# Attention with mixture-of-experts routing: reciprocals brought across partitions by a product, q scaled while it is split, loads, stores and scatters at other places of a pair, last routing in other banks

## The chip, the cores and the metric

One core of a Trainium2 chip runs the whole program. The metric is the device time of one execution, in microseconds (us); the time of a kernel is the median of its runs. Five engines work beside each other: PE (TensorE), DVE (VectorE), ACT (ScalarE), POOL (GpSimd) and SP (SyncE), which here only issues DMAs. Each engine takes its instructions strictly in the order of its own list.

## The reference

```
scores = scale * q @ k.T + bias(|i - j|, i)      # 8 batches x 8 heads, 576 x 576, head size 64
attn   = exp(scores - max) / (sum + 1e-9)
x      = (attn @ v), as 4608 tokens x 512        # token = (batch, position), heads side by side
logits = x @ w_gate + modality_bias[modality]    # 8 experts
e      = argmax(logits); g = softmax(logits)[e]
out    = g * (relu(x @ w1[e]) @ w2[e])           # 512 -> 1024 -> 512, the token's own expert
```

All is float32. The kernel splits operands into a high part (fp32r) and the rest, and adds three products.

## The kernel before, in words

**Stages.** A first stage of about 78 us builds the bias table. Then `attention` goes over 32 pairs of heads (four pairs make a batch), up to about 625 us. Then `moe_first` and `moe_rest` multiply tiles of 256 tokens by their expert's weights, in a phase of products with w1 and one with w2.

**A pair.** `ORDER` is a table of five strings, the stages 0 to 4 of a pair's turn n; `attention` carries the words out in that order, and this order in the program is the order on each engine. A `+` means pair n+1, `++` pair n+2, a `-` pair n-1. `S` issues score products of 128 queries (`scores`), `E` the exponentials on ACT, `T` transposes, `A` products with v, `R` and `N` the remaining 64 positions, `C` a copy on POOL that keeps them (L458). A capital starts a step on PE and the small letter copies its banks out. `L` issues the q and k loads on SP (L359, L363), `Q` is `scale_q`, which multiplies q by -1/8 in place on POOL (L386), `V` loads v (L372, L378). `P` transposes q and k on PE into the banks `x`, `H` writes the high part on ACT (`high`), `G` the rest on DVE (`low`). The remaining 64 rows of q, in `QD`, already take the factor -1/8 in `high` and `low` (L336, L343), while the other rows are copied with factor 1 (L334, L341).

**Routing beside attention.** From stage 2 of every fourth turn (n = 5, 9, 13, ...) the words `Y`, `X` and `O` carry out a batch's steps of `route_steps`, one batch behind. `s_recip` takes reciprocals of the softmax sums (`rs`, DVE) and spreads them over `rec` by POOL copies (L771, L776). The sums of the last 64 positions lie for one head of a pair in partitions 64 to 127 and are wanted in 0 to 63: POOL copies them to `mv` (L778), SP issues a DMA from `mv` to `mv2` (L780), and POOL copies `mv2` into `rec` (L798). `s_logits` multiplies by the gate's weights (L790, into `eps`, copied out at L327 and L329), `s_logits_t` transposes the result into the banks `x`, and DVE multiplies it by `rec` (L814, `lw`). `s_rows` transposes x rows into the banks `x`; ACT and DVE copy them to one of two row buffers `xrb`, POOL multiplies by `rec` (L905), and `D` (`route_store`) has SP store them to `xg` in DRAM (L946). `s_scatter`, by the word `Z`, is an indirect DMA from POOL that writes token numbers to `tab` (L922), five for each batch. A scatter waits until the one before has landed.

**Routing beside experts.** The last batch's routing runs in `moe_first`, between products. Its banks `x` are `xps`, which are also two of the three banks `p2` that the second phase of a tile (L1283) and the transposes of the next tile's rows (`xprep`, L1247) take in turn. Two other banks, `pq`, are used by `tiny` in `moe_rest` alone.

Of the kernel before, what the change touches and what calls it, by code (L numbers as in the profile page):

```python
# [11 lines left out]
F32 = mybir.dt.float32  # L12
# [4 lines left out]
ALU = mybir.AluOpType  # L17
# [4 lines left out]
P = 128  # L22
S = 576
D = 64
H = 8
NP = H // 2
HID = 32
S4 = S // 4
HS = S // 2
E = 8  # L30
DM = H * D
# [78 lines left out]
class Attn:  # L110
# [269 lines left out]

    SC = float(-1.0 / np.sqrt(np.float32(D)))

    def scale_q(self, n):

        x = self.qraw[n].rearrange("p c h d -> p (c h d)")
        self.nc.gpsimd.tensor_scalar(x, x, self.SC, None, op0=ALU.mult)  # L386

    def prep(self, n, part, u="x"):

        QK, QD, bk = self.QK[n % 2], self.QD[n % 2], self.banks[u]  # L390
        if part < 2:
            x = (self.qraw, self.kraw)[part].pop(n)
            for j in range(4):
                self.turn(bk, 64 * j, x[:, j, :, :].rearrange("p h d -> p (h d)"))
            hi, lo = (QK[:, part, a, 0:512].rearrange("p (j r w) -> p j r w", j=4, r=2) for a in range(2))
            return [
                (bk[r][:, 0:256].rearrange("p (j w) -> p j w", j=4), hi[:, :, r], lo[:, :, r], 1.0) for r in range(2)
            ]
        x = self.qkrem[n % 2]
        self.turn(bk, 256, x[:, 0, :])  # L400
        self.nc.tensor.transpose(bk[0][:, 320:384], x[0:64, 1, :], self.idf[0:64, 0:64])
        out = [(bk[r][:, 256:320], QD[:, 0, 64 * r : 64 * r + 64], QD[:, 1, 64 * r : 64 * r + 64], self.SC) for r in range(2)]
        return out + [(bk[0][:, 320:384], QK[:, 1, 0, 512:S], QK[:, 1, 1, 512:S], 1.0)]
# [138 lines left out]
    def first_steps(self, route):  # L542


        out = {}

        def add(blk, f):
            out.setdefault(blk, []).append(f)

        def pe(k):  # L550
            evac[k] = self.prep(0, k)

        def split(parts):
            for x in parts:
                self.high(*x)
                self.low(*x)

        evac = {}
        add(0, lambda: self.load_qk(0))
        add(self.V0, lambda: self.load_v(0))  # L560
        add(self.TG1[0], lambda: self.nc.sync.dma_start(self.tg1, self.io["c_tg1"]))
        add(self.TG1[1], lambda: self.nc.scalar.activation(self.tg1, self.tg1, AF.Copy, scale=self.w1c[:, 0:1]))
        add(self.PREP0[0] - 2, lambda: self.scale_q(0))
        for blk, k in zip(self.PREP0, (0, 1, 2)):
            add(blk, lambda k=k: pe(k))
            add(blk + 1, lambda k=k: split(evac.pop(k)))
        if self.n_pair > 1:
            loads = self.qk_loads(1)
            for blk in self.QK1:
                add(blk, lambda: next(loads, None))  # L570
        for blk in self.ROUTE:
            add(blk, lambda: next(route, None))
        return out
# [4 lines left out]


    ORDER = (  # L580
# [5 lines left out]
    )  # L586

    def attention(self):
        n_pair = self.n_pair
        tail = self.first_tiles() if self.K else {}  # L590
        for at in self.ROUTE_LATE:
            tail.setdefault(at, []).append(lambda: next(self.route, None))
        for u, k in self.LATE:
            tail.setdefault((0, u), []).append(lambda k=k: next(self.late[k], None))
        self.bg = None
        scored, evac = {}, {}
        half = lambda k: lambda u: [(u, b, k) for b in range(2)]
        bank = lambda k: lambda u: [(u[0], int(u[1]), k)]
        high = lambda u: half(1)(u) + half(2)(u)
        both = self.both = lambda u: half(0)(u) + high(u)  # L600
        steps = {
            "T": (self.etrans, lambda u, c: half(0)(u) if c == 4 else both(u)),
            "R": (self.rtrans, high),
            "N": (self.rtrans4, bank(2)),
            "A": (self.av, lambda u, k: bank(0)(u)),
            "P": (self.prep, lambda u, k: (high if k == 2 else half(0))(u)),
        }

        def start(k, n, *a):
            f, parts = steps[k]  # L610
            self.hold((k, n, *a[:-1]), parts(a[-1], *a[:-1]))
            evac[(k, n, *a[:-1])] = f(n, *a)

        def end(k, n, *a):
            a, by = (a[:-1], ["av".index(a[-1])]) if a and isinstance(a[-1], str) else (a, [])
            evac.pop((k, n, *a))(*by)
            del self.held[k, n, *a]

        def low(n, k):
            for x in evac.pop(("P", n, k)):  # L620
                self.low(*x)
            del self.held["P", n, k]

        pair = {
            "S": lambda n, c: scored.update({(n, c): self.scores(n, c)}),
            "E": lambda n, c: self.exps(*scored[n, c].pop(0)),
            "C": self.compact,
            "H": lambda n, k: [self.high(*x) for x in evac["P", n, k]],
            "G": low,
            "Q": self.scale_q,  # L630
            "V": lambda n: n in self.vmain or self.load_v(n),
            "L": self.load_qk,
        }
        for k in steps:
            pair[k] = lambda *a, k=k: start(k, *a)
            pair[k.lower()] = lambda *a, k=k: end(k, *a)
        for n in range(n_pair + 2):
            for u in range(5):
                for f in tail.get((n, u), ()):
                    f()  # L640
                if u == 2 and n > 1 and n % NP == 1:
                    assert self.route_done()
                    self.bg = self.route_steps(n // NP - 1)
                for op in self.ORDER[u].split():
                    op, _, to = op.partition(":")
                    m = n + op.count("+") - op.count("-")
                    if op == "D":
                        self.route_store()
                    elif op == "Z":
                        self.route_scatter()  # L650
                    elif op in ("X", "Y", "O"):
                        self.route_next(op, to)
                    elif op in ("x", "y"):
                        self.route_evac(op.upper())
                    elif 0 <= m < n_pair and not (n > n_pair and op[0] in "CV"):
                        pair[op[0]](m, *(int(x) for x in op[1:].strip("+-")), *([to] if to else []))
        while self.scatters:
            self.route_scatter()
# [96 lines left out]
    def route_steps(self, b):  # L755
        nc, rt = self.nc, self.rt
        xT = [self.xT[NP * b + p] for p in range(NP)]
        sums = [self.sums.pop(NP * b + p) for p in range(NP)]
        rec, oh = self.rec, self.oh
        C5 = [P, 5, E]  # L760
        st = {}
# [4 lines left out]
        def s_recip():  # L766
            rs = rt.tile([P, NP, 9], F32, tag="rs", name=f"rs{b}")
            for p in range(NP):
                nc.vector.tensor_scalar(rs[:, p, :], sums[p], 1e-9, None, op0=ALU.add)
            nc.vector.reciprocal(rs, rs)  # L770
            nc.gpsimd.tensor_copy(  # L771
                rec[:, 0:4, :].rearrange("p c (n h) -> p c n h", h=2),
                rs[:, :, 0:8].rearrange("p n (c h) -> p c n h", h=2),
            )
            r4 = rec[:, 4, :].rearrange("p (n h) -> p h n", h=2)
            nc.gpsimd.tensor_copy(r4[0:64, 0, :], rs[0:64, :, 8])  # L776
            mv = rt.tile([P, NP], F32, tag="mv", name=f"mv{b}")
            nc.gpsimd.tensor_copy(mv, rs[:, :, 8])  # L778
            mv2 = rt.tile([64, NP], F32, tag="mv2", name=f"mv2{b}")
            nc.sync.dma_start(mv2, mv[64:P, :])  # L780
            st["mv2"] = mv2

        def s_logits(u):
            st["lt"] = self.lt if b == self.B - 1 else next(self.xr_next)
# [3 lines left out]
            for cols, ps, _ in parts:  # L788
                for p in range(NP):
# [5 lines left out]
                        stop=True,  # L795
                        tile_position=(0, 32 * p),
                    )
            nc.gpsimd.tensor_copy(rec[0:64, 4, :].rearrange("p (n h) -> p h n", h=2)[:, 1, :], st["mv2"])  # L798

            def out():  # L800
                for k, (_, ps, dst) in enumerate(parts):
                    self.copy(k, dst, ps)

            return out

# [221 lines left out]
    def moe_tiles(self, st):  # L1027
# [6 lines left out]
        self.mo = [mp.tile([P, DM], F32, name=f"mo{k}") for k in range(2)]  # L1034
        pp = st.enter_context(tc.tile_pool(name="mps", bufs=1, space=PSUM))
        self.p1 = [pp.tile([P, 2, TS], F32, name=f"p1{k}") for k in range(3)]
        self.pq = [pp.tile([P, DM], F32, name=f"pq{k}") for k in range(2)]
        self.p2 = [pp.tile([P, DM], F32, name="p2")] + self.xps
        self.at = {"p2": -1}

# [609 lines left out]
```

## Time and profile before

| | |
|---|---|
| median of 3 runs | 1106.6 us (1103.4 to 1108.98) |
| the profiled execution, its own time | 1111.95 us |
| its span, first to last instruction | 1110.2 us, granted PE clock 0.970 |
| PE busy | 1018.1 us (92%) |
| DVE, ACT, POOL busy | 748.0 (67%), 683.5 (62%), 266.3 us (24%) |

A PE that is busy 92% of the span leaves some 90 us in which it waited. The profile lists instructions by their line in the program, what an engine waited for before an instruction ("idle before, releaser"), and the clock that PE was granted, where 1.00 is 2.4 GHz and 0.50 is 1.2 GHz.

### The profile page before, as it was taken

Reading aid. Unit: us, or ns where it says so; the run is one execution under the profiler, and the core shown is the slowest. Engines: PE = TensorE matmul, PEld = TensorE weight load, DVE = VectorE, ACT = ScalarE, POOL = GpSimd, SP = SyncE. Lnnn points to the kernel's source line nnn. Section 1 sums busy time; section 2 is a strip of 40 time slices with the busy share of each in tenths; the row PEclk is TensorE's granted clock in tenths of the full one; section 3 lists DMA queues with packets and bytes.
Section 4 is the critical chain, followed back from the end, with each engine's and each line's share of the span. In section 5 each row is a group of like instructions: output and inputs, shape, how many; then the busy total and the mean of one; then the engine's idle time right before and its main releaser. Section 6 shows DMA issues by size and latency. Waiting matters only on the chain. (4 is left out here: it accounts for less than half of the span.)

```text
span 1110.2 us, 30041 instructions
## 1 busy us (share of the span) xinstructions
PE 1018.1 (92%) x11590; PEld 853.6 (77%) x11590; DVE 748.0 (67%) x1777; ACT 683.5 (62%) x1576; POOL 266.3 (24%) x419
## 2 busy tenths in 40 slices
PE   6989999979799798998998888899999999999996
PEld 3447878868688687786876776788978789988995
DVE  7977778858678586886887455777445445565554
ACT  6768778858678576776876544444544445555443
POOL 1012223323233233232323321331302022111120
PEclk9999999989999899898998998999999999999999
DMA  6953222433322332223327101121545712111111
GB/s 173 212 129 75 63 48 75 65 59 105 60 64 61 63 94 49 75 68 66 94 40 221 46 20 39 39 64 48 175 157 190 251 46 63 53 39 48 39 54 36
DMA packets 125677, 93.52 MB, mean 84 GB/s; under 512 B 94737, under 2 KB 103313, under 8 KB 125524
## 3 DMA queue, kind: packets, MB, share of 16 engines
q1 hardware_dynamic: 117908, 71.20, 24.8%
q0 software_dynamic: 7520, 20.30, 6.0%
q8 instruction: 94, 1.54, 0.8%
q14 instruction: 59, 0.48, 0.2%
q10 hardware_dynamic: 96, 0.00, 0.0%
HBM read 141.40 MB, written 19.38 MB: 145 GB/s over the span
## 5 line engine op out<-in xcount | busy, mean ns | idle before, releaser
L453 ACT ACTIVATE Eb<-Eb,mn 128x576 f32<-128x576 f32 x288 | 224.6, 787 | 46.0 <-DVE mn L439 45.8
L439 DVE CUSTOM_DVE_ANT_0 Eb<-sps,NBm 128x576 f32<-128x576 f32 x256 | 183.5, 754 | 21.0 <-PE sps L416 15.3
L416 PE MATMUL sps<-QK 64*128 64x288 f32 x1536 | 153.9, 319 | 11.7 <-ACT QK L334 6.0
L528 PE MATMUL eps<-eT,vraw 128*64 128x144 f32 (+2 forms) x2048 | 158.3, 298 | 6.6 <-ACT eT L327 5.7
L1266 PE MATMUL p<-QK,w1hi 128*128 128x256 f32 x1152 | 162.8, 284 | 1.2 <-ACT w1hi L1239 1.2
L1266 PEld LDWEIGHTS p<-QK,w1hi 128*128 128x128 f32 x1152 | 149.1, 192 | 7.8 <-issue 5.0
L528 PEld LDWEIGHTS eps<-eT,vraw 128*64 128x64 f32 x2048 | 123.3, 140 | 31.9 <-ACT eT L327 16.6
L416 PEld LDWEIGHTS sps<-QK 64*128 64x128 f32 x1536 | 118.2, 193 | 24.7 <-DVE QK L341 10.0
L1269 DVE SCALAR_TENSOR_TENSOR hl<-p,hh 128x512 fp32r<-128x512 f32 x72 | 49.7, 690 | 127.9 <-ACT hh L1268 127.9
L329 DVE COPY eT<-eps 128x512 f32<-128x512 f32 x128 | 87.8, 686 | 49.5 <-PE eps L322 45.7
L1268 ACT ACTIVATE hh<-p 128x512 fp32r<-128x512 f32 x72 | 43.0, 597 | 124.9 <-PE p L1266 112.9
L1292 POOL DMA_INDIRECT out<-mo,idt x36 | 36.5, 1014 | 297.0 <-ACT mo L1291 283.3
L1233 DVE TENSOR_TENSOR w2lo<-NBm,w2hi 128x1024 fp32r<-128x1024 f32 x72 | 89.3, 1240 | 16.2 <-ACT w2hi L1232 16.1
L322 PE MATMUL eps<-idf,Eb 64*128 64x64 f32 x2048 | 94.8, 230 | 4.8 <-ACT xTb L327 1.8
L458 POOL COPY rem<-Eb 128x128 f32<-128x128 f32 x128 | 37.2, 291 | 255.7 <-ACT Eb L453 226.8
L1283 PE MATMUL xps<-w2hi,hh 128*128 128x512 f32 x208 | 86.6, 416 | 7.3 <-DVE NBm L329 3.7
L1266 PE MATMUL p<-QK,w1lo 128*128 128x256 f32 x576 | 92.7, 283 | 0.2 <-DVE w1lo L1240 0.2
L322 PEld LDWEIGHTS eps<-idf,Eb 64*128 64x128 f32 x2048 | 81.8, 143 | 9.8 <-ACT xTb L327 4.3
L1233 DVE TENSOR_TENSOR w1lo<-NBm,w1hi 128x1024 fp32r<-128x1024 f32 x72 | 84.9, 1220 | 3.3 <-ACT w1hi L1232 1.1
L1283 PE MATMUL xps<-w2hi,hl 128*128 128x512 f32 x208 | 84.3, 405 | 0.0
L327 ACT COPY eT<-eps 128x512 f32<-128x512 f32 x128 | 77.4, 605 | 4.6 <-PE eps L322 2.1
L1266 PEld LDWEIGHTS p<-QK,w1lo 128*128 128x128 f32 x576 | 79.4, 192 | 0.6 <-DVE w1lo L1240 0.6
(244 smaller groups left out, 1810.8 us busy)
## 6 DMA issues: line engine op xcount, KB each, us to landing
NBm<-moe_w SPq DMA_DIRECT2D x20, 2048.0 KB
NBm<-moe_w SPq DMA_DIRECT2D x40, 1024.0 KB
NBm<-moe_w SPq DMA_DIRECT2D x32, 512.0 KB
NBm<-xTb SPq DMA_DIRECT2D x32, 288.0 KB
qraw<-q SPq DMA_DIRECT2D x64, 128.0 KB
kraw<-k SPq DMA_DIRECT2D x64, 128.0 KB
vraw<-v SPq DMA_DIRECT2D x32, 256.0 KB
xg<-xrb SPq DMA_DIRECT2D x28, 258.0 KB
```

The costliest lines, as they stand in the source:

```text
L322: self.nc.tensor.transpose(ps[r][0:n, col : col + 64], x[o, :], self.idf[o, o])
L327: self.nc.scalar.copy(out, ps)
L329: self.nc.vector.tensor_copy(out, ps)
L416: nc.tensor.matmul(self.sps[h or 0][:, half, 0:HS], QD[:, a, :] if h is None else QK[o, 0, a, P * c : P * c + P], QK[o, 1, b, ks], start=i ...
L439: nc.vector.tensor_tensor_reduce(out=e.rearrange("p (t w) -> p t w", t=2), in0=ps, in1=nb.rearrange("p (t w) -> p t w", t=2), scale=1.0, s ...
L453: self.nc.scalar.activation(e, e, AF.Exp, bias=mn, scale=-1.0, accum_out=sm)
L528: nc.tensor.matmul(ps[o, :], v[:, h, k, :] if k < 4 else self.vrem[n % 2][:, o], eT[:, h, k, sl] if k < 4 else rT[:, sl], start=k == 0, st ...
L1233: self.nc.vector.tensor_tensor(l, w, h.bitcast(F32), op=ALU.subtract)
L1266: nc.tensor.matmul(ps[:, a, :], w[:, c, fs], x[:, c, :], start=i == 0, stop=i == len(ops) - 1)
L1268: nc.scalar.activation(hh[:, sl, :], ps, AF.Relu)
L1269: nc.vector.scalar_tensor_tensor(hl[:, sl, :], ps, 0.0, hh[:, sl, :].bitcast(F32), op0=ALU.max, op1=ALU.subtract)
L1283: nc.tensor.matmul(ps, h[:, f, sl], m[:, f, :], start=i == 0, stop=i == len(ops) - 1)
```

## The change

`scale_q` is gone; `prep` hands the factor -1/8 for q to `high` and `low`. The word `Q+` in stage 0 is replaced by `L++`, which stood at the head of stage 4. The two `D` of stages 1 and 3 become one at the end of stage 4. `Z` in stage 4 scatters only if all five scatters of a batch are waiting, or in the last turns. `mv`, `mv2` and their copies and DMA are replaced by a product in `s_logits`: columns 64 to 127 of the identity as weights, the four columns of `rs` as the other operand, which puts partitions 64 to 127 into rows 0 to 63 of a bank; DVE copies that into `rec`. In `moe_first` the banks `x` are the two `pq`.

```diff
-    def scale_q(self, n):
-        x = self.qraw[n].rearrange("p c h d -> p (c h d)")
-        self.nc.gpsimd.tensor_scalar(x, x, self.SC, None, op0=ALU.mult)
...
-                (bk[r][:, 0:256].rearrange("p (j w) -> p j w", j=4), hi[:, :, r], lo[:, :, r], 1.0) for r in range(2)
+                (bk[r][:, 0:256].rearrange("p (j w) -> p j w", j=4), hi[:, :, r], lo[:, :, r], (self.SC, 1.0)[part]) for r in range(2)
...
-        add(self.PREP0[0] - 2, lambda: self.scale_q(0))
...
-        "T2-:e t2- S0 Q+ A2--:e0 a2--:a Y:e1 y X:x E0 T3-:e",
-        "x t3- S1 A3--:e0 N-:e1 E0 E1 n- D E1 a3--:v T4-:x R-:x T0:e C0 C1 Z r-:a O",
+        "T2-:e t2- L++ S0 A2--:e0 a2--:a Y:e1 y X:x E0 T3-:e",
+        "x t3- S1 A3--:e0 N-:e1 E0 E1 n- E1 a3--:v T4-:x R-:x T0:e C0 C1 Z r-:a O",
         "t4-:a t0 S2 O A0-:e1 a0-:a E2 P2+:x E2 P0+:x",
-        "H2+ T1:e H0+ V t1 S3 E3 D C2 G0+ A1-:e1",
-        "L++ a1-:v E3 S4 P1+:x H1+ G1+ G2+ O Z C3 O E4",
+        "H2+ T1:e H0+ V t1 S3 E3 C2 G0+ A1-:e1",
+        "a1-:v E3 S4 P1+:x H1+ G1+ G2+ O Z C3 O E4 D",
...
                     elif op == "Z":
-                        self.route_scatter()
+                        if u < 4 or n > n_pair - 3 or len(self.scatters) == 5:
+                            self.route_scatter()
...
-            mv = rt.tile([P, NP], F32, tag="mv", name=f"mv{b}")
-            nc.gpsimd.tensor_copy(mv, rs[:, :, 8])
-            mv2 = rt.tile([64, NP], F32, tag="mv2", name=f"mv2{b}")
-            nc.sync.dma_start(mv2, mv[64:P, :])
-            st["mv2"] = mv2
+            st["rs"] = rs
...
-            nc.gpsimd.tensor_copy(rec[0:64, 4, :].rearrange("p (n h) -> p h n", h=2)[:, 1, :], st["mv2"])
+            odd = self.banks[u[0]][1 - k][0:64, 384 : 384 + NP]
+            nc.tensor.matmul(odd, self.idf[:, 64:P], st["rs"][:, :, 8], start=True, stop=True, tile_position=(0, 0))
+            dst4 = rec[0:64, 4, :].rearrange("p (n h) -> p h n", h=2)[:, 1, :]
...
                     self.copy(k, dst, ps)
+                self.copy(1, dst4, odd)
...
-        self.pq = [pp.tile([P, DM], F32, name=f"pq{k}") for k in range(2)]
+        self.pq = self.banks["x"] = [pp.tile([P, DM], F32, name=f"pq{k}") for k in range(2)]
```

**POOL, turns 9 and 10, where a batch's routing begins beside the scatters of the batch before.** Each row is a line of the program, the operation, and tile<-tiles with partitions x elements. First the kernel before:

```order
L922 DMA tab<-ids,pos_3161 36992x1
L771 COPY rec<-rs_3475 128x32
L776 COPY rec<-rs_3475 64x4
L778 COPY mv_3483<-rs_3475 128x4
L458 COPY rem_2_3555<-Eb 128x128
L922 DMA tab<-ids,pos_3161 36992x1
L458 COPY rem_3_3605<-Eb 128x128
L386 TENSOR_SCALAR qraw_3569<-qraw_3569 128x512
L798 COPY rec<-mv_3485 64x4
L458 COPY rem_0_3763<-Eb 128x128
```

The same place with the change (L915 is the scatter, L765 and L770 the copies into `rec`, L453 the copy of `C`):

```order
L915 DMA tab<-ids,pos_3156 36992x1
L765 COPY rec<-rs_3470 128x32
L770 COPY rec<-rs_3470 64x4
L453 COPY rem_2_3546<-Eb 128x128
L453 COPY rem_3_3585<-Eb 128x128
L453 COPY rem_0_3754<-Eb 128x128
```

Between the copies of turn 9 and that of turn 10 POOL had a scatter, the scaling of a loaded q and the last copy into `rec`; now it has only copies of `C`.

**SP, the same turns.** Before, from the store of a batch's last rows in turn 9:

```order
L946 DMA xg<-xrb_93 64x516
L780 DMA mv_3485<-mv_3483 64x4
L372 DMA vraw_3532<-v 128x2x256
L378 DMA vrem_114<-v 64x64 x2
L359 DMA qraw_3569<-q 128x4x64 x2
L363 DMA qkrem_116<-q 64x64 x2
L359 DMA kraw_3574<-k 128x4x64 x2
```

Now (L939 is the store); the q loads ahead of this piece are those that stood behind it:

```order
L359 DMA kraw_3314<-k 128x4x64 x2
L363 DMA qkrem_116<-k 64x64 x2
L372 DMA vraw_3523<-v 128x2x256
L378 DMA vrem_114<-v 64x64 x2
L939 DMA xg<-xrb_93 64x516
L359 DMA qraw_3607<-q 128x4x64 x2
```

The DMA of `mv` is gone, the store stands behind the loads of v, and q and k of two turns ahead come four stages earlier.

**PE, beside the experts: the ranks of the last batch (L862, L863) and the second phase of a tile (L1283).** Before:

```order
L862 MATMUL xps_77<-ohb,tri 128x48
L863 LDWEIGHTS ones
L863 MATMUL xps_77<-ohb,ones 128x48
L1283 MATMUL xps_77<-w2hi,hh 128x512
L1283 MATMUL xps_77<-w2hi,hl 128x512
```

Now (L855, L856 and L1276 are the same lines):

```order
L855 MATMUL pq_10644<-ohb,tri 128x48
L856 LDWEIGHTS ones
L856 MATMUL pq_10644<-ohb,ones 128x48
L1276 MATMUL xps_77<-w2hi,hh 128x512
L1276 MATMUL xps_77<-w2hi,hl 128x512
```

The routing's product and the tile's product wrote the same bank one behind the other; now they write different ones. The order on PE is otherwise the same.

## Rows read from the trace of the kernel before

**Rows 1.** The table of stretches: from and to in us, length, busy time of PE, PEld (weight loads), DVE, ACT and POOL with their instructions, then the granted PE clock, the DMA engines' share and GB/s. Two stretches of attention and two pieces of the second.

```profile
170.00:216.00 46.00, 44.71 (x749) 38.48 (x747) 38.69 (x119) 37.67 (x115) 16.43 (x31) 1.00 0.28 71
216.00:242.00 26.00, 19.13 (x277) 15.72 (x273) 13.79 (x41) 13.51 (x40) 4.76 (x8) 0.87 0.52 70
...
232.00:235.00 3.00, 2.26 (x31) 1.96 (x33) 2.88 (x8) 1.58 (x5) 0.00 (x0) 0.50 0.65 166
238.00:241.00 3.00, 2.99 (x58) 2.58 (x56) 2.01 (x7) 2.18 (x9) 0.26 (x1) 1.00 0.06 3
```

**Rows 2.** The timeline of PE: start and length in us of the score products with `QD`, which come once in a turn. The turns 5 and 6, the turns 8, 9 and 10, and the last two of the kind 29 and 30.

```profile
153.50 1.06 PE L416 MATMUL sps<-QK,QD 128*128 128x288 f32 x6
170.29 1.07 PE L416 MATMUL sps<-QK,QD 128*128 128x288 f32 x6
...
201.53 1.06 PE L416 MATMUL sps<-QK,QD 128*128 128x288 f32 x6
216.74 1.06 PE L416 MATMUL sps<-QK,QD 128*128 128x288 f32 x6
242.07 1.06 PE L416 MATMUL sps<-QK,QD 128*128 128x288 f32 x6
...
573.91 1.05 PE L416 MATMUL sps<-QK,QD 128*128 128x288 f32 x6
597.37 1.06 PE L416 MATMUL sps<-QK,QD 128*128 128x288 f32 x6
```

**Rows 3.** The list of waits of the whole span: who waited for whom, total us, times, longest.

```profile
POOL qraw L386 <- DMA qraw<-q: 75.3, 9, 19.3
...
DVE lw L814 <- POOL rec L798: 44.9, 7, 8.2
...
PE eps L504 <- DVE eT L329: 24.7, 6, 5.9
```

**Rows 4.** The timeline of the second batch's wait, all engines: start us, us, instruction, and in brackets the idle time of its engine before it with the releaser.

```profile
214.97 0.49 SPq L780 DMA_DIRECT2D mv<-mv  x1
...
217.36 1.26 SPq L359 DMA_DIRECT2D qraw<-q  x2
...
229.84 1.49 POOL L386 TENSOR_SCALAR qraw<-qraw 128x512 f32<-128x512 f32 x1 [7.38 <-DMA qraw<-q]
231.29 0.18 POOL L798 COPY rec<-mv 64x4 f32<-64x4 f32 x1
...
231.50 0.56 DVE L814 TENSOR_TENSOR lw<-xps,rec 128x160 f32<-128x160 f32 x2 [8.15 <-POOL rec L798]
...
232.71 0.48 PE L504 MATMUL eps<-idf,Eb 128*64 128x64 f32 x4 [5.88 <-DVE eT L329]
```

**Rows 5.** The timeline of PE beside the experts: the instructions before which it waited, with the wait and its releaser.

```profile
656.02 1.09 PE L1247 MATMUL xps<-idf,NBr 128*128 128x128 f32 x8 [3.64 <-DVE lw L814]
...
677.37 0.47 PE L1283 MATMUL xps<-w2hi,hh 128*128 128x512 f32 x1 [2.15 <-DVE rks L870]
...
686.73 0.46 PE L322 MATMUL xps<-idf,xTb 64*128 64x64 f32 x7 [0.93 <-DVE QK L1251]
...
688.65 0.80 PE L1283 MATMUL xps<-w2hi,hh 128*128 128x512 f32 x1 [1.47 <-ACT NBm L327]
...
709.87 0.50 PE L1283 MATMUL xps<-w2hi,hh 128*128 128x512 f32 x1 [1.30 <-DVE NBm L329]
...
718.19 0.46 PE L322 MATMUL xps<-idf,xTb 64*128 64x64 f32 x8 [1.70 <-DVE QK L1251]
...
721.03 0.79 PE L1283 MATMUL xps<-w2hi,hh 128*128 128x512 f32 x1 [2.37 <-DVE NBm L329]
```

**Rows 6.** The table of stretches, as rows 1, for the first tiles.

```profile
675.00:690.00 15.00, 10.41 (x44) 8.10 (x44) 8.33 (x12) 6.37 (x9) 1.03 (x1) 0.83 0.05 17
690.00:720.00 30.00, 25.66 (x174) 22.46 (x173) 18.32 (x41) 13.07 (x19) 11.12 (x11) 0.96 0.20 45
720.00:760.00 40.00, 38.97 (x243) 34.97 (x244) 31.66 (x91) 15.78 (x22) 11.67 (x14) 0.93 0.19 57
```

**Rows 7.** Groups of instructions by line with shapes kept apart: out<-in, shapes, count | busy us in all, mean ns of one | idle before.

```profile
L343 DVE SCALAR_TENSOR_TENSOR QD<-xps,QD 128x64 fp32r<-128x64 f32 x64 | 11.0, 213 | 1.0 <-ACT QD L336 1.0
L336 ACT ACTIVATE QD<-xps 128x64 fp32r<-128x64 f32 x64 | 10.2, 212 | 0.0
L504 PE MATMUL eps<-idf,Eb 128*64 128x64 f32 x128 | 10.2, 241 | 24.7 <-DVE eT L329 24.7
...
L334 ACT CAST QK<-xps 128x64 fp32r<-128x64 f32 x32 | 6.9, 215 | 0.2 <-DVE QD L343 0.2
L341 DVE TENSOR_TENSOR QK<-xps,QK 128x64 fp32r<-128x64 f32 x32 | 6.8, 212 | 0.1
```

**Rows 8.** The start of attention: eight stores of the bias table's last part on SP, the loads behind them, and the first use on DVE.

```profile
63.63 9.77 SPq L219 DMA_DIRECT2D NBr<-xTb  x8
73.51 1.28 SPq L359 DMA_DIRECT2D qraw<-q  x2
...
79.34 0.75 DVE L439 CUSTOM_DVE_ANT_0 Eb<-sps,NBr 128x576 f32<-128x576 f32 x1
```

**Rows 9.** A store of rows on SP in an undisturbed turn, and two stretches behind it (columns as rows 1).

```profile
193.92 2.23 SPq L946 DMA_DIRECT2D xg<-xrb  x2
...
204.00:206.00 2.00, 1.89 (x26) 1.60 (x26) 1.86 (x8) 0.90 (x3) 0.83 (x1) 1.00 0.05 7
206.00:208.00 2.00, 1.95 (x41) 1.56 (x38) 1.31 (x6) 1.27 (x5) 0.00 (x0) 1.00 0.00 0
```

More of the change, by code (lines that the diff above doesn't have):

```diff
@@ L629, in attention @@
             "G": low,
-            "Q": self.scale_q,
             "V": lambda n: n in self.vmain or self.load_v(n),
```

## The prediction, before the changed kernel ran

> **What bounds the kernel now.** I read the page's busy shares first: PE works 92% of the span, so whatever the change gives has to come out of the 92 us in which PE stands, or out of stretches where it runs at half clock. Work taken from POOL, SP or DMA counts only where PE waits for it. So I next looked at where PE stands.
>
> The table of stretches and the starts of the score products tell this for the attention. In an undisturbed stretch PE is busy 44.71 of 46 us at clock 1.00; in the 26 us from 216 on it is busy 19.13 at a mean clock of 0.87 [rows 1]. The product with `QD` comes once in a turn, so the distance of two is a turn's length: 15.21 us from 201.53 to 216.74, but 25.33 for the next one [rows 2]. That one is the turn in which a batch's routing begins. There are six such long turns, one for each batch from the second on; the last has 23.46. In the first batch the same routing work gives a turn of 16.79 (153.50 to 170.29), so the routing itself costs 1.6 us and the rest of the long turns is a stall.
>
> The list of waits names the stall: DVE waits 44.9 us in 7 places for POOL's copy into `rec`, PE waits 24.7 us in 6 places for DVE's copy of `eT`, and POOL waits 75.3 us for q's loads [rows 3]. The timeline of one place puts these in a chain [rows 4]. q's load was issued at 217.36; POOL's `scale_q` gets it at 229.84, 12.5 us later. POOL's list is in order, so the small copy of `mv2` into `rec` stands behind it and runs at 231.29, although its own DMA was issued at 214.97, ahead of q's. DVE's product `lw` waits 8.15 us for that copy, DVE's later copies of `eT` stand behind `lw`, and PE's transposes wait 5.88 us for them. After the wait PE first runs at half clock: 0.50 in 232 to 235, and 1.00 again in 238 to 241 [rows 1]. So the wait is for q, not for the DMA that carries the reciprocals. Two numbers agree on its size: the mean wait of PE is 24.7/6 = 4.1 us, and a mean clock of 0.87 over 26 us means 2 x 0.13 x 26 = 6.8 us at half clock, which loses half of that, 3.4; together 7.5 us. The turns give (25.33 + 23.46)/2 - 16.79 = 7.6.
>
> Beside the experts, the timeline of PE shows seven waits while the last batch is routed: 3.64, 2.15, 0.93, 1.47, 1.30, 1.70 and 2.37 us, 13.6 in all [rows 5]. Each is in front of a product that writes a bank `xps`, and the releaser is an engine that still reads that bank for the routing (`lw`, `rks`, `NBm`) or for the tile. In these stretches the clock is 0.83, 0.96 and 0.93 [rows 6].
>
> **The change part by part.**
>
> *`scale_q` goes, `mv` becomes a product.* Either edit alone breaks the chain at another link; together POOL has no wait for q, and `lw` needs only PE and DVE. Gain: 6 x 7.6 = 45 us. The seventh wait of `lw` (last batch) is the 3.64 of rows 5 and is counted there.
>
> *The factor -1/8 in `high` and `low`.* For the same shape ACT takes 212 ns with the factor and 215 without, DVE 213 and 212 [rows 7]. Cost 0.
>
> *Eight added products and eight DVE copies.* The nearest product of four-byte data in `eps` takes 241 ns at the most for 64 columns [rows 7]; with 4 columns it is less, and never below nothing. Eight cost 0 to 1.9 us; I take 1. The copy has 64x4 elements, fewer than the 212 ns copies of rows 7, and stands ahead of a `lw` that also waits for the transposes after it, which hide it; without that cover it adds at most 8 x 0.2 = 1.7.
>
> *`L++` four stages earlier, `V` no longer behind `mv` and stores.* Loads start most of a 15-us turn sooner than in rows 4, and what they took there was 12.5. On SP they pass the V loads and the stores; `L++` overwrites raw q and k that were transposed in the turn before, so SP has nothing new to wait for. At the start of the attention two turns' q and k loads now stand among the bias table's last stores, four issues of some 1.28 us, 5.1 in all. The stores end at 73.40, and DVE first uses the result at 79.34, 5.9 us later [rows 8]. The cost is 0 to 5; since the slack is the larger, I take 0.
>
> *Stores and scatters.* One scatter a turn instead of up to two: POOL's wait for the landing of the one before shrinks, and POOL no longer holds anything up. I take 0. A store of rows at the turn's end instead of its middle lets go of its row buffer later; ACT's and DVE's next copies into that buffer wait for it. In an undisturbed turn the store was issued at 193.92 and the DMA engines were at 0.05 by 204 to 206 and idle in 206 to 208 [rows 9]: at most 12 us, loads behind it included. Now V's loads and their wait stand ahead of the store, while the q and k loads that used to stand behind it have gone before, and the next copies into the buffer come in stage 1 of the next turn, behind a whole group of 128 queries. I take 0; the other end is the third rival.
>
> *Banks `pq` in `moe_first`.* The routing's products write other banks than the tile's, so the seven waits have no cause: 13.6 us. The stretches of rows 6 hold 2 x (0.17 x 15 + 0.04 x 30 + 0.07 x 40) = 13.1 us at half clock, which costs at most 6.6; I take 5, as some may have causes that stay.
>
> Sum: 45 + 13.6 + 5 - 1 = 62.6. The profiled execution took 1111.95 and would take 1049; the median, 5.35 lower, would be 1044. Some of those 5.35 us can lie in the very stalls that go, so I forecast **1046 us**.
>
> **The rivals.**
>
> *Only the attention's part comes back.* In `moe_first` a tile still needs its rows, its two `p2` banks and DVE's copies; the routing's chain of small DVE steps may hold DVE when the tile's copies are due, and each wait on a bank becomes one on a copy. For it: three of the seven releasers are plain copies of the tile (`QK`, `NBm`). Against it: those copies are late because the bank was handed over late. It keeps 45 - 1 = 44: 1106.6 - 44 = 1063. Chance 0.16.
>
> *The stall moves on.* If q's landing is what is slow, PE's transposes of q wait in the place of POOL. In the chain of rows 4 that would need the loads to land a turn later than they did there, though issued sooner; or the copies of `rec` stay behind a scatter that lands late, and `lw` waits as before. Then the attention keeps its long turns and the new loads only add traffic; what the experts give is spent there. 1105 us, no change. Chance 0.03.
>
> *Row buffers come free too late (slower).* A store that follows V's loads, at the end of a turn, could still be reading its buffer when ACT and DVE want to overwrite it; both are in order, and PE waits for their copies. There are two such places in a batch, 14 in the attention. Each us of lateness costs 14; past (62 + 5.5)/14 = 4.8 us at each the kernel is slower than before. With 6 us: 1106.6 - 62 + 84 = 1128. For it: a store can take up to the 12 us of rows 9, and in the long turns the DMA engines are busy at 0.65 [rows 1]. Against it: in the undisturbed turn the DMA engines had nothing left after 206. The Trainium skill ("DMA: Bandwidth & Descriptors", Queues, rings and completion order) says that each DMA engine consumes the descriptors of one issuer's row in ring order; by that a store behind V's loads starts only when they have been read. The bound from rows 9, where the loads stood behind the store, has no such delay in it. Chance 0.05.
>
> **How the numbers follow.** The forecast has 0.76: its own range is 1036 (all terms at their better end, and what the slower profile hides) to 1056 (the clock term nothing, product and copies in full, and SP's 5 us at the start). The range given reaches on to the first rival, 1068, and leaves out the other two. About 0.5%, 5.5 us, is what a measurement can tell from no change here. Faster: 0.76 + 0.16 = 0.92; no change 0.03; slower 0.05.
>
> **What would show it.** Right: turns after a routing's beginning of about 17 us, no wait of DVE's `lw` for POOL, none of PE for `eT`, clock 1.00 through the attention, no PE wait above 1 us in front of an `xps` product between 650 and 720 of the old time scale, and less half clock there. Wrong: long turns that stay (second rival), copies into `xrb` that wait for a DMA (third), PE waits in `moe_first` with a new releaser (first), or DVE's first use of the bias table later than now.

## The result and the profile after

The changed kernel takes 1063.6 us (median of 4 runs, 1062.8 to 1065.3) against 1107.8 us: a ratio of 0.960, 95% interval 0.956 to 0.965. It is faster by 44 us where 61 were forecast. The profiled execution took 1065.25, its span is 1063.5 us at a granted PE clock of 0.988. Beside the runs b1 to b4 of the experiments six of the eleven runs of the kernel before were slow ones, over 1.5% above the fastest, and against the median of the other five, 1105.0 us, the ratios of b1 to b4 come to 0.970, 0.965, 0.976 and 0.960.

From the first to the last product with `QD` the profile before took 535.1 us and the one after 506.7; from the last product to the end 496.9 and 479.5. So 28.4 us came from the attention and 17.4 from what follows it.

**Beside the experts** the table of stretches (columns as [rows 1]) shows this, where [rows 6] had clocks of 0.83, 0.96 and 0.93:

```profile
646.00:661.00 15.00, 15.00 (x101) 13.04 (x100) 7.33 (x11) 6.31 (x10) 4.21 (x5) 1.00 0.14 53
661.00:691.00 30.00, 29.23 (x211) 26.24 (x210) 27.32 (x71) 14.67 (x21) 13.77 (x15) 1.00 0.26 56
691.00:731.00 40.00, 39.73 (x243) 34.98 (x242) 32.09 (x68) 21.36 (x28) 8.36 (x9) 1.00 0.19 56
```

The clock is 1.00 in all three. Of the seven waits of [rows 5] none is left; PE waits over 0.5 us in two places there, for other engines:

```profile
643.29 0.18 PE L856 MATMUL pq<-ohb,ones 128*128 128x48 bf16 x1 [0.91 <-DVE ohb L842]
...
672.37 0.50 PE L1276 MATMUL xps<-w2hi,hl 128*128 128x512 f32 x1 [0.77 <-DVE hl L1262]
```

**In the attention** the list of waits has no DVE `lw` waiting for POOL (44.9 us in [rows 3]) and no `eps` transposes waiting for `eT`; `lw` now waits for PE alone, at most 0.6 us:

```profile
DVE lw L807 <- PE xps L322: 4.3, 7, 0.6
```

The timeline of the products with `QD` answers to [rows 2] (L411 is its L416). Here are those of the turns 0 and 1, 9 to 12, and 30 and 31; a turn's length is the distance from the product of the turn before:

```profile
77.28 1.06 PE L411 MATMUL sps<-QK,QD 128*128 128x288 f32 x6 [0.83 <-DVE mn L434]
96.55 1.06 PE L411 MATMUL sps<-QK,QD 128*128 128x288 f32 x6
...
220.62 1.05 PE L411 MATMUL sps<-QK,QD 128*128 128x288 f32 x6
237.75 1.05 PE L411 MATMUL sps<-QK,QD 128*128 128x288 f32 x6
257.17 1.05 PE L411 MATMUL sps<-QK,QD 128*128 128x288 f32 x6
272.68 1.06 PE L411 MATMUL sps<-QK,QD 128*128 128x288 f32 x6
...
567.15 1.05 PE L411 MATMUL sps<-QK,QD 128*128 128x288 f32 x6
583.98 1.06 PE L411 MATMUL sps<-QK,QD 128*128 128x288 f32 x6
```

Turn 10 takes 17.13 us in place of 25.33. The six long turns together take 104.7 us instead of 145.2. But turn 1 takes 19.27 us where it took 14.59, and turn 11 19.42 where it took 15.76. That is where gain was given back: 4.7 and 3.7 us, and some 4 more in the turns 19, 20 and 31. Of the six, turn 30 still has 19.30 us, the others 16.9 to 17.3.

Turn 1 first. The timelines of SP, DVE and PE at the start of the attention (after; compare [rows 8]):

```profile
63.95 3.61 SPq L219 DMA_DIRECT2D NBr<-xTb  x4
67.66 1.31 SPq L359 DMA_DIRECT2D qraw<-q  x2
...
73.57 2.55 SPq L219 DMA_DIRECT2D NBr<-xTb  x4
```

```profile
80.65 0.76 DVE L434 CUSTOM_DVE_ANT_0 Eb<-sps,NBr 128x576 f32<-128x576 f32 x1 [2.07 <-POOL xrb L703]
...
81.56 0.40 PE L411 MATMUL sps<-QK 64*128 64x288 f32 x2 [1.97 <-DVE mn L434]
```

```profile
80.00:84.00 4.00, 2.26 (x26) 2.07 (x27) 2.74 (x9) 1.34 (x3) 0.12 (x2) 0.79 0.69 118
84.00:88.00 4.00, 3.83 (x36) 2.93 (x36) 2.84 (x8) 2.42 (x6) 0.29 (x1) 0.50 0.42 92
88.00:92.00 4.00, 3.84 (x46) 3.38 (x43) 1.58 (x4) 2.99 (x10) 0.29 (x1) 0.50 0.02 2
```

The last stores of the bias table are issued until 76.12 instead of 73.40. DVE's first use of them then waits 2.07 us, until 80.65, 4.5 us behind the end of the last issue (the releaser named, a POOL memset of another tile, had been done for 0.5 us by then). PE waits 1.97 us, and then runs at half clock through 84 to 92. In turn 11 the place is another:

```profile
238.73 0.46 PE L322 MATMUL xps<-idf,kraw 64*128 64x64 f32 x8
239.03 0.66 PE L322 MATMUL eps<-idf,Eb 64*128 64x64 f32 x16
242.36 1.12 PE L411 MATMUL sps<-QK 64*128 64x288 f32 x4 [2.67 <-ACT QK L334]
```

```profile
241.66 0.65 ACT L334 CAST QK<-xps 128x256 fp32r<-128x256 f32 x2 [2.51 <-remote]
```

PE's transposes of k are recorded at 238.73 to 239.2, but ACT, which waits for them, starts at 241.66, and SP's next load of k, which waits for the same transposes, is issued at 241.69. The trace names no releaser on the core.

### The profile page after: what moved, and what is told of

It is laid out like the page before. It is cut to its first block, busy times and chain, and to the rows that moved or that the text cites. A ratio compares the mean times of both kernels' runs of the same rounds, so it can differ in the third digit from the quotient of the medians.

```text
span 1063.5 us, 29967 instructions
## 1 busy us (share of the span) xinstructions
PE 1003.6 (94%) x11606; PEld 843.5 (79%) x11606; DVE 749.6 (70%) x1785; ACT 683.5 (64%) x1576; POOL 216.1 (20%) x371
## 5 line engine op out<-in xcount | busy, mean ns | idle before, releaser
L411 PE MATMUL sps<-QK 64*128 64x288 f32 x1536 | 151.6, 316 | 16.0 <-ACT QK L334 7.4
L411 PEld LDWEIGHTS sps<-QK 64*128 64x128 f32 x1536 | 115.8, 190 | 29.1 <-ACT QK L334 10.9
L329 DVE COPY eT<-eps 128x512 f32<-128x512 f32 x128 | 88.0, 688 | 44.4 <-PE eps L322 40.5
L453 POOL COPY rem<-Eb 128x128 f32<-128x128 f32 x128 | 37.3, 292 | 337.4 <-ACT Eb L448 291.8
L1276 PE MATMUL xps<-w2hi,hh 128*128 128x512 f32 x208 | 83.0, 399 | 0.0
L1276 PE MATMUL xps<-w2hi,hl 128*128 128x512 f32 x208 | 81.4, 392 | 0.8 <-DVE hl L1262 0.8
```

The source lines that it names most:

```text
L329: self.nc.vector.tensor_copy(out, ps)
L411: nc.tensor.matmul(self.sps[h or 0][:, half, 0:HS], QD[:, a, :] if h is None else QK[o, 0, a, P * c : P * c + P], QK[o, 1, b, ks], start=i ...
L1276: nc.tensor.matmul(ps, h[:, f, sl], m[:, f, :], start=i == 0, stop=i == len(ops) - 1)
```

## The experiments

One or more edits each, in words or as a diff. The ratio is to the kernel before, run beside it on the same chip; its median there was 1105.7 to 1112.9. The groups a, b, c and d ran on four different chips, so ratios are what to compare between groups. "Attention" is the time from the first to the last `QD` product in the profiled execution, "rest" that from there to the end; the profiled execution can lie some us off the median (b3's took 1085.8, a3's 1085.0).

| kernel | median us | ratio, 95% interval | attention | rest |
|---|---|---|---|---|
| before | 1107.8 | 1 | 535.1 | 496.9 |
| changed | 1063.6 | 0.960 (0.956 to 0.965) | 506.7 | 479.5 |
| changed, again (a1) | 1060.4 | 0.957 (0.953 to 0.961) | 503.4 | 478.2 |
| changed, first loads late (a2) | 1053.9 | 0.952 (0.948 to 0.955) | 494.5 | 476.8 |
| before + banks (a3) | 1090.7 | 0.986 (0.981 to 0.992) | 527.5 | 478.8 |
| before + no scale_q (a4) | 1082.2 | 0.977 (0.973 to 0.982) | 505.3 | 494.0 |
| before + product (b1) | 1071.4 | 0.966 (0.959 to 0.972) | 501.2 | 492.0 |
| before + both of these (b2) | 1066.5 | 0.960 (0.953 to 0.967) | 497.2 | 493.1 |
| three edits: b2 + banks (c1) | 1054.4 | 0.950 (0.946 to 0.953) | 492.7 | 478.9 |
| c1 + scatters as changed (c2) | 1054.2 | 0.948 (0.944 to 0.951) | 499.3 | 477.4 |
| c1 + stores as changed (c3) | 1070.6 | 0.964 (0.959 to 0.969) | 507.2 | 479.0 |
| changed, all loads late (b3) | 1078.1 | 0.970 (0.965 to 0.975) | 529.0 | 478.6 |
| a2, stores and scatters as before (b4) | 1060.4 | 0.956 (0.951 to 0.961) | 507.1 | 477.1 |
| a2, one scatter moved (d1) | 1058.5 | 0.958 (0.953 to 0.962) | 499.3 | 477.1 |

**The start of the attention.** The changed kernel once more:

> The changed kernel once more, for its own spread and for a second profile. Theory A (the profile after shows what every execution does): the median is 1063.6 within 1.5 us, turn 1 takes 19.3 us again, and the turns 11 and 19 take 19.4 and 18.5 us again. Theory B (the long turns 11 and 19 are single events of the one profiled execution): turn 1 takes 19.3 us again, but turns 11 and 19 take 15.8 us and others may be long in their place.

Measured 1060.4; turn 1 took 19.60 us again, turn 11 19.95, but turn 19 15.75; turn 20 was long in its place (19.06). So A holds for the turns 1 and 11, B for 19.

```diff
+                    if op == "L++" and (n == 0) != (u == 4):
+                        continue
...
-        "a1-:v E3 S4 P1+:x H1+ G1+ G2+ O Z C3 O E4 D",
+        "L++ a1-:v E3 S4 P1+:x H1+ G1+ G2+ O Z C3 O E4 D",
```

> The changed kernel, but in turn 0 the q and k loads of pair 2 stand at the head of stage 4, as in the kernel before, and not among the last stores of the bias table. Theory A (the loads delay the stores, DVE then waits 2.07 us for the table's last part, PE 1.97, and PE's half clock after it costs the rest): turn 1 goes from 19.27 to 14.6 to 15.2 us, the time falls by 4 to 4.7 us to about 1059. Theory B (the wait at 80.65 is for POOL's memset or for the order of DVE, not for the stores): turn 1 stays at 19 us and the time at 1063.

Measured 1053.9, beside 1060.4 for the changed kernel on the same chip: 6.5 us less, with only the order of SP's loads and stores in turn 0 changed. Turn 1 is back at 14.61 us, and the clock stays at 1.00 where it fell (the products of the turns 0 and 1, then the stretches):

```profile
77.40 1.06 PE L411 MATMUL sps<-QK,QD 128*128 128x288 f32 x6 [0.83 <-DVE mn L434]
92.01 1.06 PE L411 MATMUL sps<-QK,QD 128*128 128x288 f32 x6
```

```profile
80.00:84.00 4.00, 3.41 (x42) 2.53 (x42) 3.41 (x11) 2.81 (x7) 0.24 (x2) 1.00 0.43 95
84.00:88.00 4.00, 3.13 (x61) 2.76 (x62) 2.59 (x6) 3.54 (x12) 0.59 (x2) 1.00 0.49 68
```

A holds. The runs of the two kernels lie apart (1050.6 to 1055.8 and 1058.7 to 1062.9). Turn 1 itself accounts for 4.7 to 5.0 of the 6.5 us; where the rest was is not shown. Turn 11 stays long (19.84), so early first loads have no part in that.

**The banks.** `self.pq = self.banks["x"] = [...]` in the kernel before:

> The kernel before with one edit: the banks x are the two pq in moe_first. Theory A (the part beside the experts is worth 17.4 us by the two profiles, and independent of the rest): 1107.8 - 17 = 1090 to 1091, the seven waits of PE between 655 and 722 gone but the one that lw's wait for POOL made, since the last batch's copy of mv2 still stands on POOL. Theory B (the waits there need the earlier routing of the whole change): 1100 to 1107.

Measured 1090.7, 17.9 us less: A. By the profiles "rest" falls by 18.1 us (496.9 to 478.8), and none of the seven waits of [rows 5] is left, not even the one that A expected to stay. "Attention" is 7.6 us shorter there as well, though its program is the same: turn 14 took 17.00 us in that execution, and 24.58 in that of the kernel before. The stall of a long turn is thus not there every time, which is taken up below.

**The chain of the long turns, link by link.** First without `scale_q`:

> The kernel before with one edit: no scale_q, the factor -1/8 in high and low. mv, its DMA and the order of loads stay. Theory A (only q's landing in front of POOL's copy made the long turns): the six turns go from 24.2 to about 17 us, 1107.8 - 43 = 1065 to 1069, as much as the whole attention part of the change. Theory B (the DMA of mv, or a scatter ahead of the copy, lands nearly as late as q): lw still waits 2 to 6 us for POOL, turns of 19 to 22 us, 1080 to 1095.

Measured 1082.2: B's range. `lw` waits for POOL once (5.9 us, the last batch), so neither theory's wait is there. Instead PE waits for loads of k, which are late themselves, 3.1 us in two places (timelines of SP and PE, turn 10):

```profile
214.08 0.49 SPq L778 DMA_DIRECT2D mv<-mv  x1
...
216.48 1.26 SPq L359 DMA_DIRECT2D qraw<-q  x2
...
220.63 0.57 SPq L359 DMA_DIRECT2D kraw<-k  x1
```

```profile
232.02 0.27 PE L401 MATMUL xps<-idf,qkrem 64*128 64x64 f32 x1 [2.14 <-DMA qkrem<-k]
```

The other long turn, 18 (21.76 us), has no such wait; DVE waits 3.44 us there without a releaser on the core, of which more at the end. Then the product alone, with `scale_q` kept:

> The kernel before with one edit: mv, its DMA and POOL's copies are replaced by the product in s_logits; scale_q stays on POOL, the loads stay late. Theory A (the chain of the long turns breaks at either link, as the prediction said; what then stays is PE's own wait for late q and k): lw waits for no POOL copy, the six turns take 17 to 22 us, and the time is that of the kernel without scale_q, 1082, within 6 us. Theory B (scale_q itself holds q back, so PE's transposes of q wait for POOL in the place of lw): turns of 20 to 24 us, 1092 to 1105.

Measured 1071.4, better than either theory. Without the DMA of `mv` on its list SP issues the loads of the same turn sooner:

```profile
207.72 0.48 SPq L945 DMA_DIRECT2D xg<-xrb  x1
208.30 2.89 SPq L372 DMA_DIRECT2D vraw<-v  x1
...
212.44 1.26 SPq L359 DMA_DIRECT2D qraw<-q  x2
...
215.06 1.27 SPq L359 DMA_DIRECT2D kraw<-k  x2
```

Turn 9's product with `QD` starts at 215.85 in the kernel without `scale_q` and at 215.10 here, so q is issued 2.7 us ahead of it instead of 0.6 behind it. POOL's wait for q falls from 75.3 us [rows 3] to 28.7, none of it in front of `lw`. Then both:

> Both edits of the chain (no scale_q, product in the place of mv), loads, stores, scatters and banks as in the kernel before. Theory A (without scale_q alone what is left is PE's wait for late loads, 2.14 us for qkrem in one place; the DMA of mv costs nothing more): 1082 again, within 4 us, and turns of 20 us stay where PE waits for a load. Theory B (the DMA of mv on SP's list and its landing were the other half of the stall): 1067 to 1072, all six turns at 17 us.

Measured 1066.5: B, with five of the six turns at 16.8 to 17.7 us and turn 30 at 19.4. The order of the three says that the DMA of `mv` cost more than `scale_q`. Its place on SP's list is a reason: it waited for POOL's copy into `mv`, and V's, q's and k's loads stood behind it. The list of waits of the kernel before has this wait of SP:

```profile
SPq L780 <- POOL mv L778: 39.5, 7, 11.8
```

POOL's copy in turn waited for DVE's reciprocals: they end at 214.41, POOL's copies start at 214.48, after 1.29 us of idle time. The scatter ahead of them on POOL's list was issued by 213.18.

A late issue is not the whole of the stall. In turn 5 of the kernel before, the first with a routing, q is issued as late as in turn 9, 0.6 us behind the turn's product, and yet turn 6 takes only 16.79 us: q lands within 4.4 us (timelines of SP and POOL).

```profile
154.12 1.26 SPq L359 DMA_DIRECT2D qraw<-q  x2
...
158.52 1.49 POOL L386 TENSOR_SCALAR qraw<-qraw 128x512 f32<-128x512 f32 x1 [3.19 <-DMA qraw<-q]
```

What turn 5 lacks is the scatters of a batch before. In all six long turns POOL gets q 8.7 to 9.7 us after it started a scatter, however long before that q was issued (6.8 to 12.5 us). Turn 14 says more, in the kernel before (first pair, 24.58 us) and in the one with the banks alone (second pair, 17.00 us):

```profile
292.47 1.26 SPq L359 DMA_DIRECT2D qraw<-q  x2
...
300.30 1.49 POOL L386 TENSOR_SCALAR qraw<-qraw 128x512 f32<-128x512 f32 x1 [7.58 <-DMA qraw<-q]
```

```profile
289.52 1.26 SPq L359 DMA_DIRECT2D qraw<-q  x2
...
294.20 1.49 POOL L386 TENSOR_SCALAR qraw<-qraw 128x512 f32<-128x512 f32 x1 [1.60 <-DMA qraw<-q]
```

POOL starts a scatter at 291.43 and 291.31. Issued 1.0 us behind it, q takes 7.8 us; issued 1.8 us ahead of it, 4.7 us, and there is no stall. Meanwhile the DMA engines are busy at only 0.04 to 0.22 from 292 to 298 in the kernel before, so the amount of data does not explain it. That a scatter under way holds the load back fits all of this, but no run leaves the scatters out: this rival, and with it the share of the late issue, stays open.

**The three edits without the new order.**

> The kernel before with the three edits that take waits away (no scale_q, the product in the place of mv, the banks pq for the routing in moe_first) and with its own order of loads, stores and scatters. Theory A (the new order of the change gives back part of what these three bring): 1066.5 of the two edits of the chain, less 17 to 18 of the banks, is 1048 to 1051, faster than the changed kernel by 10 to 14 us. Theory B (the gains overlap, or the early loads are needed): 1058 or more.

Measured 1054.4 (1049.9 to 1058.9): 0.8 to 1.1% below the changed kernel by the ratios, whose intervals lie apart or just touch (0.946 to 0.953 against 0.956 to 0.965 and 0.953 to 0.961). That is A in kind, though 3 us short of its range. The six long turns take 16.8 to 17.0 us, 101.2 in all, and turn 1 14.58, but turn 19 18.44; turn 10 as an example (products of the turns 9, 10 and 11):

```profile
215.06 1.06 PE L416 MATMUL sps<-QK,QD 128*128 128x288 f32 x6
231.87 1.06 PE L416 MATMUL sps<-QK,QD 128*128 128x288 f32 x6
247.90 1.06 PE L416 MATMUL sps<-QK,QD 128*128 128x288 f32 x6
```

**The new order, piece by piece.** All loads at their old place in the changed kernel:

> The changed kernel with L++ back at the head of stage 4 in every turn; product, factor, stores, scatters and banks as changed. Theory A (the early loads are worth what PE's waits for loads cost, some 2 to 4 us in four to six turns, and cost 5 to 6 us at the start): turn 1 takes 14.6 us, some of the six long turns take 18 to 21 us with PE waiting for q or k, and the time is 1060 to 1068. Theory B (the early loads give nothing and are what makes turn 11 long): turn 11 takes 15.8 us, the six turns 17 us, and the time is 1050 or less.

Measured 1078.1, slower than either theory says. ACT waits for a store of rows (timelines of SP and ACT):

```profile
194.66 1.27 SPq L359 DMA_DIRECT2D qraw<-q  x2
...
200.02 1.71 SPq L939 DMA_DIRECT2D xg<-xrb  x2
```

```profile
210.45 0.36 ACT L327 COPY xrb<-xps 64x256 f32<-64x256 f32 x1 [4.37 <-DMA xg<-xrb]
```

The stores stand behind q's and k's loads here, so this one is issued at 200.02, 0.2 us behind its turn's product, where the changed kernel issues it at 200.56, 4.8 us ahead of that product; what ACT copies at 210.45 could have gone at 206. That is the prediction's third rival. The store's landing is not a matter of data still to be moved, for the DMA engines are nearly idle while ACT waits (columns as [rows 1]):

```profile
206.00:208.00 2.00, 0.93 (x16) 0.69 (x12) 0.00 (x0) 0.07 (x1) 0.00 (x0) 1.00 0.06 4
208.00:210.00 2.00, 0.00 (x0) 0.00 (x0) 0.00 (x0) 0.00 (x0) 0.00 (x0) 1.00 0.00 1
```

The rival is tried alone by moving `D`, on the three edits:

```diff
-        "x t3- S1 A3--:e0 N-:e1 E0 E1 n- D E1 a3--:v ...
-        "H2+ T1:e H0+ V t1 S3 E3 D C2 G0+ A1-:e1",
-        "L++ a1-:v E3 S4 P1+:x H1+ G1+ G2+ O Z C3 O E4",
+        "x t3- S1 A3--:e0 N-:e1 E0 E1 n- E1 a3--:v ...
+        "H2+ T1:e H0+ V t1 S3 E3 C2 G0+ A1-:e1",
+        "L++ a1-:v E3 S4 P1+:x H1+ G1+ G2+ O Z C3 O E4 D",
```

> The three edits, and of the new order the place of the stores alone (once, at the end of a turn). Theory A (the third rival of the prediction: with loads late, the store stands behind q's and k's loads and lands after the next copy into its row buffer): ACT and DVE wait 2 to 5 us for the store in two places of a batch, turns 9, 12, 17, 21 take 20 to 22 us, and the time is 20 to 30 us above the three edits alone, 1070 to 1080. Theory B (the waits come from the scatters' new places instead): within 3 us of the three edits alone.

Measured 1070.6, 16 us above the three edits on the same chip: A in kind, less in size than the 20 to 30 expected. The turns 9, 17 and 29 were long (21.3, 19.3 and 21.2 us), 12 and 21 only 16.1 and 16.3. The list of waits:

```profile
DVE xrb L329 <- DMA xg<-xrb: 16.3, 8, 5.4
ACT xrb L327 <- DMA xg<-xrb: 11.0, 7, 4.4
```

In the changed kernel these two lines are 1.7 and 1.4 us, once each: with the loads four stages earlier the store no longer stands behind them. The rule for scatters alone:

> The three edits, and of the new order the rule for scatters alone (one in a turn, as changed). Theory A (POOL no longer holds anybody up, so the place of a scatter is worth nothing): within 2 us of the three edits alone. Theory B (two scatters in a turn slow the loads of q and k that are late here): 3 to 6 us less than the three edits alone, and the turns 10, 11 and 18 shorter than 17.1 to 17.7 us.

Measured 1054.2 against 1054.4: A. Yet in its profile turn 11 takes 20.32 us, with the loads late. And the other way round, early loads with the old places of stores and scatters:

> The changed kernel with pair 2's loads late (median 1053.9 in the runs before this) and, on top of it, the stores D and scatters Z at their places in the kernel before. Theory A (the places of stores and scatters are worth nothing): 1054 within 2 us, turn 11 again at 19.8 us. Theory B (they keep transfers out of the way of q and k, or a scatter makes turn 11 long): 3 us or more either way, and turn 11 changes.

Measured 1060.4, so B's size: with early loads the new places look worth some 6 us. But the two kernels ran on different chips, and the intervals of their ratios overlap (0.948 to 0.955 and 0.951 to 0.961), so the gain is not shown clear of noise. Turn 11 takes 16.58 us here, but the turns 10, 15, 18 and 31 take 19 to 21.

**Turn 11.**

```diff
-                        if u < 4 or n > n_pair - 3 or len(self.scatters) == 5:
+                        if (n, u) == (11, 4) or (u < 4 and n != 10) or n > n_pair - 3 or len(self.scatters) == 5:
```

> The changed kernel with pair 2's loads late, and one of its 35 scatters in the attention moved: the one that is issued 4.6 us before the end of turn 10 goes to the end of turn 11. Turn 11 took 19.4 to 20.3 us in all four profiles in which that scatter stood there with the new rule for scatters in place. Theory A (the scatter is still under way while q's loads start, and PE's results of those microseconds reach ACT and SP only when it has landed): turn 11 takes 15.8 us, the time falls by 4 us to about 1050, and turn 12 may be longer by 1 us. Theory B (the place in the program or in memory does it, not the scatter): turn 11 takes 19.8 us again and the time stays at 1054 within 1.5 us.

The products of the turns 10, 11 and 12:

```profile
233.09 1.05 PE L411 MATMUL sps<-QK,QD 128*128 128x288 f32 x6
248.95 1.05 PE L411 MATMUL sps<-QK,QD 128*128 128x288 f32 x6
266.80 1.05 PE L411 MATMUL sps<-QK,QD 128*128 128x288 f32 x6
```

Turn 11 takes 15.86 us, as A says, but turn 12 17.85, and the turns 20, 26 and 30 are 1.0 to 2.5 us longer too than with that scatter in its place: the median is 1058.5 where A had 1050. In turn 12 DVE waits 2.53 us, until 261.09, 8.2 us after POOL started a scatter. The scatter's place decides whether that one turn is long, and the stall moved with it. How a scatter would make PE's results come late is not shown, and what is saved at one turn was lost at others.

## Why the prediction was off, point by point

The forecast was 1046 with an own range of 1036 to 1056. The lower end goes too far: the terms at their better end give 45 + 13.6 + 6.6 = 65.2, so about 1041, and 1036 takes the 5.35 us of the slower profile off a second time. The measured 1063.6 lies outside this range, and inside the range given only because that was drawn out to the first rival's 1068, whose mechanism did not occur.

**The long turns** (45 us): right. The three edits have 44.0 there by the profiles (145.2 to 101.2), the changed kernel 40.5 and, in its second profile, 44.3. "Either edit alone breaks the chain": right in kind, since both did, by 26 and by 34 to 42 us. But "the wait is for q, not for the DMA that carries the reciprocals" was half of it. I looked at what ended POOL's wait, and not at why q's load was issued as late as 217.36; [rows 4] had part of the answer in its first line, the DMA of `mv` at 214.97, behind which SP's list had stood. Nor did I ask why q took 12.5 us to land there, and 4.4 at the same place of turn 5, where no scatter runs.

**The factor, the products, the copies** (0, 1, 0): not measured apart. The profiled c1 took 1049.9 us, 62.1 less than the profiled execution of before, against a sum of 62.6. So close a match is luck in part, for this c1 was the shortest of its six; by the medians the three edits bring 56.7 us.

**The banks** (13.6 + 5): right; 17.9 by the medians with that edit alone, 17.4 by the profiles of before and after.

**`L++` at the start** (0 taken, 0 to 5 the bounds): this step failed. It cost 4.7 to 5.0 us in turn 1, 6.5 by the medians. I set 5.1 us of SP's issues against 5.9 us between the last store's issue and the first use [rows 8]. But a store isn't done when it is issued: its data still had to land. In the changed kernel DVE, which had waited, went on 4.5 us behind the last issue, so of the 5.9 only some 1.4 was slack. The stores were 2.7 us later and DVE waited 2.07, which is the sign of being wrong that the prediction names last. The second part of the miss is that a wait of 1.97 us was followed by some 10 us with PE at half clock, as [rows 1] had shown for a wait of 5.88.

**Loads, stores and scatters otherwise** (0): right only for the three together, and leaving aside the single long turns. Without the start's cost the new order is worth nothing against the old one (0.952 and 0.950). One by one they are not nothing: the stores alone cost 16 us, through the wait that the third rival names, and the early loads make them harmless. I priced the store against the buffer's next copy, but with the loads already moved, which is why it came out at nothing. I also took idle DMA engines for a store that has landed [rows 9]; with all loads late the engines were nearly idle from 206 on, and ACT was let go at 210.45. And "SP has nothing new to wait for" was wrong: the loads of q and k (L359) wait 99 us for PE in the changed kernel, against 0.5 before, most of it for transposes. No cost of that shows by itself, as PE waits for no load of q or k there.

**The sum** was for one execution without single stalls. The profiled c1 is nearly that; the median of the three edits lies 4.5 us above it, 5.0% below before instead of the 5.5% of the forecast. Of the 17.6 us missing in the changed kernel, the start has 4.7 to 6.5 and turn 11 some 4; the rest the profiles show only in part, as single longer turns that are others in each profile.

**The rivals.** The first one's time came out (1063) by coincidence, not by its mechanism: beside the experts all came back. The second appears in part, without the early loads: PE waited for k itself. The third's wait is real, and was avoided only by the early loads.

## What to carry to other kernels

Follow a late load back to its issue, and ask what the issuing engine's list stood at before it: a tiny DMA that waits for another engine holds every load behind it (39.5 us in seven places here). Then ask why it takes so long to land, and compare a turn where it does not. Slack for a store ends at its landing, not at its issue, and a wait of PE can cost more than its length when the clock falls behind it: 4.7 us here for 1.97. Edits of an order that look free one by one belong together: measure the removals of waits without the new order first, since here they alone beat the whole change by 0.8 to 1.1%.

## What was not expected

In single turns PE's results reach the other engines late: in turn 11 of four profiles ACT waited 2.51 to 3.03 us for transposes that PE's records have long ended, with a scatter and q's loads under way. It is not peculiar to the changed order. In eight of the fourteen profiles the attention has eleven places where ACT or DVE waits over 1 us without a releaser on the core, 1.7 to 3.4 us each: two are in the changed kernel's first profile, others in the kernels without `scale_q` and with the product alone. All eleven end 8.1 to 11.1 us after POOL started a scatter. Where POOL itself waited for a scatter to land, that took 4.8 to 10.9 us from its start. So the release falls in with the landing of a scatter, as q's does in the long turns of the kernel before, and moving the scatter moved the stall. Whether the scatter, the loads or something else beside the core holds the results back stays open; no run here separates them.
